# Holding the conversion and the fetch of a block of weights behind one more instruction of the step before

## The chip, the cores and the metric

The kernel runs on one core of one Trainium2 chip. That core has five engines that work side by side, each through its own list of instructions in its own order: TensorE (PE, matrix products), VectorE (DVE), ScalarE (ACT), GpSimd (POOL) and SyncE (SP, which here only issues transfers). The metric is the device time of one execution in microseconds (us), lower is better. Before the change it is 1103.98 us, the median of three runs (1102.27 to 1105.51).

## The reference

The program is an attention with a sliding window, followed by a two-layer network. There are 8 batches of 576 positions and 8 heads of 64 dimensions, so 4608 tokens of 512 numbers; everything is float32 at the output.

```
scores = q @ k.T / sqrt(64) - slope[head] * |rel|,  only where 0 <= rel < 128
attn   = exp(scores - max) / sum
x      = (attn @ v), heads side by side            # 4608 x 512
h      = x @ w_in                                  # 512 x 2048
g      = h if h >= 1;  0 if h <= -1;  (h+1)^2/4 between
out    = g @ w_out                                 # 2048 x 512
```

The two weight matrices arrive as float64. The kernel receives each of their numbers as two 32-bit words and has to put a float32 together from them before a matrix product can use it.

## The kernel before, in words

The 4608 tokens are cut into 12 chunks of 384 (`CH`); within a chunk the hidden size of 2048 is cut into 16 blocks of 128 (`NFC`), and block `fc` of chunk `c` is one step. A step does `layer1` (12 products of 128x384 into one PSUM bank `h`, then the activation: one ScalarE instruction that writes `sg`, two VectorE instructions that write `g`) and, two steps later, `layer2` (products of 128x512 that add into `acc`). The attention works by heads `m`, eight to a chunk: `scores` (products `s`, a VectorE pass at L249 that scales and takes the minimum into `z`, an exponential on ScalarE at L251, sums at L257 and L258, the fold of the two halves into `ep` at L262 or L264), `weights_t` (a transpose `p` on TensorE, a copy `lu` on ScalarE, two masks on GpSimd) and `values` (products `x`, a copy to `xn`). While the network runs on chunk `c`, the attention of chunk `c + 1` is put between its steps. The attention of chunk 0 has nothing ahead of it and stands alone at the start.

**The weights.** Block `fc` of a weight matrix is fetched by `fetch_weights(fc)`: two transfers of 512 KB that ScalarE's queue issues (L123 for `rawi`, L129 for `rawo`). `convert_in(fc)` makes the first layer's block of `rawi`, `convert_out(fc)` the second layer's of `rawo`. Both go through `float32_of`: two ScalarE instructions that scale the raw words in place (L112, L113), then three on VectorE (L114, L115, L116). `convert_in` adds a rounded copy on ScalarE (L135) and a remainder on VectorE (L136). All 16 blocks of both matrices are fetched and converted once, and must be ready for the 16 steps of chunk 0.

**What sets the order.** A scheduler writes each engine's list: of the instructions whose inputs it believes ready, it places the most urgent one first. The engines then follow their lists strictly. The only hand on it here is `behind(instructions, f)`: everything that `f` issues is placed, on the engine of each given instruction, behind that instruction. It orders one engine's list and nothing else. An instruction of `f` on an engine that has no instruction among those given is not held at all. The blocks 0 to 3 are converted behind heads of chunk 0's attention: `EARLY` names the heads, and `done_t[m]` holds the last instructions of `weights_t(m)`. The blocks 4 to 15 are converted by `convert_after`, one to a step of chunk 0: with `LEAD` = 4 it fetches block `f + 6` and converts block `f + 4` (for the second layer, behind the step before) behind `done_g[f]`, which holds instructions of the activation of step `f`.

Before the change `done_t[m]` of the first 16 heads holds a ScalarE and a GpSimd instruction, and `done_g[f]` the last VectorE instruction alone.

Of the kernel before, what the change touches and what calls it, by code (L numbers as in the profile page):

```python
# [12 lines left out]
AF = mybir.ActivationFunctionType  # L13
ALU = mybir.AluOpType
# [4 lines left out]
def windowed_attention_then_ffn(  # L19
# [21 lines left out]
    V, S, G, T, DMA = nc.vector, nc.scalar, nc.gpsimd, nc.tensor, nc.sync  # L41
# [4 lines left out]
    P = 128  # L46
# [31 lines left out]
    quarter = const.tile([P, 1], F32, name="quarter")  # L78
# [141 lines left out]
    def scores(m, blks):  # L220
        p, j = divmod(m, 2)
        c = p // NPAIR
        ql, kr, kk, kl = (pair[p].get(x) for x in ("ql", "kr", "kk", "kl"))
        if m not in head:
            head[m] = dict(ep=ap1.tile([P, NQB, P], F32, name=f"ep_{m}", tag="ep", bufs=2),
                           z=ap1.tile([P, NQB, 2 * P], F32, name=f"z_{m}", tag="z"),
                           nmax=ap1.tile([P, 4], F32, name=f"nmax_{m}", tag="nmax", bufs=2),
                           sum=sums[:, m % 2])
        st = head[m]
        nmax, sm, ep, z = st["nmax"], st["sum"], st["ep"], st["z"]  # L230
        slope = 2.0 ** -(m % H + 1)
        pt = bank(f"s_{m}_{blks[0]}").rearrange("r (m w) -> r m w", w=2 * P)
        b0 = before(c)
        win = []
        for n, i in enumerate(blks):
            lone = i + b0 == 0
            c0 = P if lone else D if c % CYCLE == 1 and i == 2 else 0
            k0 = (i + b0 - 1) * P + c0
            o = pt[:, n, c0:]
            win.append((o, c0, lone))  # L240
            if c < LIGHT:
                r, qs, ks = lo_rows[j], slice(i * P, (i + 1) * P), slice(k0, k0 + 2 * P - c0)
                T.matmul(o, ql[r, 0, qs].bitcast(F32), kr[r, 0, ks], start=True, stop=True)  # L243
                continue
            T.matmul(o, ql[:, j, i * P:(i + 1) * P], kk[:, j, k0:k0 + 2 * P - c0], start=True, stop=False)  # L245
            T.matmul(o, ql[:, j, i * P:(i + 1) * P], kl[:, j, k0:k0 + 2 * P - c0], start=False, stop=True)  # L246
        for i, (o, c0, lone) in zip(blks, win):
            r = rel_end if c % CYCLE == 1 and i == 1 else rel
            V.tensor_tensor_reduce(out=z[:, i, c0:], in0=o, in1=r[:, c0:], op0=ALU.add, op1=ALU.min, scale=-slope,  # L249
                                   scalar=3.0e38, accum_out=nmax[:, i:i + 1])  # L250
            S.activation(z[:, i, c0:], z[:, i, c0:], AF.Exp, bias=nmax[:, i:i + 1], scale=-1.0,  # L251
                         accum_out=sm[:, i, 0:1])
        if blks[-1] == NQB - 1:
            if c % CYCLE == 1:
                G.memset(z[:, 2, :D], 0.0)
            rc = st["rc"] = ap1.tile([P, 8], F32, name=f"rc_{m}", tag="rc", bufs=2)
            V.tensor_reduce(rc[:, :NQB], sm, mybir.AxisListType.X, ALU.add)  # L257
            V.reciprocal(rc[:, :NQB], rc[:, :NQB])  # L258

            for i in range(NQB):  # L260
                if i + b0 == 0:
                    V.tensor_tensor(ep[:, i, :], z[:, i, P:], rc[:, i:i + 1].broadcast_to([P, P]), ALU.mult)  # L262
                else:
                    V.tensor_tensor_reduce(out=ep[:, i, :], in0=z[:, i, :P], in1=z[:, i, P:], op0=ALU.add, op1=ALU.add,  # L264
                                           scale=rc[:, i:i + 1], scalar=0.0, accum_out=rc[:, 4 + i:5 + i])

    def weights_t(m):

        ep = head[m]["ep"]
        lu = head[m]["lu"] = ap1.tile([P, 2, 2 * NQB, P], F32R, name=f"lu_{m}", tag="lu", bufs=2)  # L270
        pt = bank(f"p_{m}")[:, :CH].rearrange("r (i w) -> r i w", w=P)
        for i in range(NQB):
            T.transpose(pt[:, i, :], ep[:, i, :], ident)  # L273
        if m < LIGHT * H:
            own = lu[:, 0, 1::2, :].bitcast(F32)
            ga = S.copy(own, pt)
            G.affine_select(out=lu[:, 0, 0::2, :].bitcast(F32), in_=own, pattern=[[0, NQB], [-1, P]],
                            base=0, channel_multiplier=1, compare_op=ALU.is_gt, fill=0.0)
            gg = G.affine_select(out=own, in_=own, pattern=[[0, NQB], [1, P]],
                                 base=0, channel_multiplier=-1, compare_op=ALU.is_ge, fill=0.0)  # L280
            done_t[m] = [ga.ins, gg.ins]
            return
        ga = S.copy(lu[:, 0, 1::2, :], pt)
        gv = V.tensor_tensor(lu[:, 1, 1::2, :], pt, lu[:, 0, 1::2, :].bitcast(F32), ALU.subtract)  # L284
        flat = lu.rearrange("p s i w -> p (s i) w")
        G.affine_select(out=flat[:, 0::2, :], in_=flat[:, 1::2, :].bitcast(F32), pattern=[[0, 2 * NQB], [-1, P]],  # L286
                        base=0, channel_multiplier=1, compare_op=ALU.is_gt, fill=0.0)
        gg = G.affine_select(out=flat[:, 1::2, :], in_=flat[:, 1::2, :].bitcast(F32), pattern=[[0, 2 * NQB], [1, P]],  # L288
                        base=0, channel_multiplier=-1, compare_op=ALU.is_ge, fill=0.0)
        done_t[m] = [ga.ins, gv.ins, gg.ins]  # L290
# [69 lines left out]
    def layer1(c, fc):  # L360
        ph = ps_h.tile([P, CH], F32, name=f"h_{c}_{fc}", tag="ps_h")
        for cc, (xh, xl) in enumerate(xs[c]):
            T.matmul(ph, wi[fc][:, 0, cc, :], xh, start=(cc == 0), stop=False)  # L363
            T.matmul(ph, wi[fc][:, 0, cc, :], xl, start=False, stop=False)  # L364
            T.matmul(ph, wi[fc][:, 1, cc, :], xh, start=False, stop=(cc == NCC - 1))  # L365

        if c == 0:
            g = gp.tile([P, CH], F32, name=f"g_{c}_{fc}", tag="gh")
        else:
            g = gp.tile([P, CH], F32, name=f"g_{c}_{fc}", tag="g", bufs=1)  # L370
        sg = gp.tile([P, CH], F32, name=f"sg_{c}_{fc}", tag="sg", bufs=1)
        S.activation(sg, ph, AF.Relu, bias=quarter[:, 0:1], scale=0.25)  # L372
        V.scalar_tensor_tensor(g, sg, 0.5, sg, ALU.min, ALU.mult)  # L373
        last = V.scalar_tensor_tensor(g, sg, -0.25, g, ALU.add, ALU.max)  # L374
        if c == 0:
            done_g[fc] = [last.ins]
            gs[c, fc] = g
            return
        gh = gp.tile([P, CH], F32R, name=f"gh_{c}_{fc}", tag="gh")
        gl = gp.tile([P, CH], F32R, name=f"gl_{c}_{fc}", tag="gl")  # L380
        S.copy(gh, g)  # L381
        G.tensor_tensor(gl, g, gh.bitcast(F32), ALU.subtract)  # L382
        gs[c, fc] = (gh, gl)
# [142 lines left out]
```

## Time and profile before

| | us |
|---|---|
| median of 3 runs | 1103.98 (1102.27 to 1105.51) |
| the profiled execution, its own time | 1102.24 |
| the span of its trace | 1100.5 |
| TensorE busy | 1045.3 (95%) |
| VectorE busy | 810.4 (74%) |
| ScalarE busy | 617.4 (56%) |
| GpSimd busy | 372.1 (34%) |

The span runs from the first instruction to the last; 1.74 us of the execution's own time lie around it. A busy share is a mean over stages that differ: the first tenth of the span, in which chunk 0's attention runs and the weights come in, looks unlike the rest. An engine's row in a timeline gives the start, the length, the line, the operation with out and in, and in brackets how long the engine stood idle before it and what ended that. The granted clock of TensorE (PEclk) is a share of its full speed.

### The profile page before, as it was taken

The numbers are of one execution on the slowest core, as the hardware profiler recorded it, in microseconds if no ns is written. First come the engines' busy times: TensorE is split into PE (matmuls) and PEld (weight loads), VectorE is DVE, ScalarE is ACT, GpSimd is POOL, SyncE is SP. The second block draws the span as 40 slices with busy tenths as digits, with TensorE's granted clock in tenths as the row PEclk, the third lists the DMA queues.
The fourth block names the chain that finished last, engine by engine and source line by source line (L and its number), as shares of the span: only waits on it lengthen the run. The fifth ranks groups of instructions, "written<-read, shape, count | busy, mean of one in ns | idle before, by whom it ended". The sixth has DMA issues, their size and how long they took to land.

```text
span 1100.5 us, 16790 instructions
## 1 busy us (share of the span) xinstructions
PE 1045.3 (95%) x5472; PEld 905.1 (82%) x5472; DVE 810.4 (74%) x2281; ACT 617.4 (56%) x1475; POOL 372.1 (34%) x419
## 2 busy tenths in 40 slices
PE   4489999999999999999999999999999999999998
PEld 2246666889899998899898898899899889899996
DVE  2458999978878878887887778897777897763322
ACT  3876335755656655655665655664665665652322
POOL 1011210433443343344344343444333444343221
PEclk9977999999999999999999999999999999999999
DMA  9722101221211312212121212211112221200000
GB/s 352 261 89 92 37 17 29 65 59 29 87 34 49 89 37 64 73 32 58 58 65 42 66 46 63 65 48 42 59 44 63 66 72 38 74 2 1 29 1 29
DMA packets 58903, 69.50 MB, mean 63 GB/s; under 512 B 4032, under 2 KB 44480, under 8 KB 58816
## 3 DMA queue, kind: packets, MB, share of 16 engines
q1 hardware_dynamic: 48064, 51.66, 16.3%
q10 hardware_dynamic: 10752, 16.78, 4.1%
q8 instruction: 43, 0.70, 0.3%
q14 instruction: 44, 0.36, 0.1%
HBM read 58.98 MB, written 9.44 MB: 62 GB/s over the span
## 4 chain that ended last, share of the span: by engine, by line
PE 80%; DVE 6%; ACT 6%; DMA 3%; issue 2%; POOL 2%; ACTq 0%; DVEq 0%; POOLq 0%
PE h L363 11%; PE h L364 11%; PE h L365 11%; PE acc L396 10%; PE acc L397 10%; PE acc L398 9%; PE x L338 5%; PE acc L393 4%; PE p L273 3%; PE s L246 2%; PE s L245 2%; PE x L314 2%; DMA rawi<-in_moe_w_in_dram 2%; PE s L243 2%; ACT z L251 1%
## 5 line engine op out<-in xcount | busy, mean ns | idle before, releaser
L382 POOL TENSOR_TENSOR gl<-g,gh 128x384 fp32r<-128x384 f32 x176 | 182.7, 1038 | 416.9 <-ACT gh L381 408.4
L363 PE MATMUL h<-xh,wi 128*128 128x384 f32 x768 | 265.9, 346 | 6.0 <-ACT xh L356 5.4
L364 PE MATMUL h<-xl,wi 128*128 128x384 f32 x768 | 261.1, 340 | 0.0
L365 PE MATMUL h<-xh,wi 128*128 128x384 f32 x768 | 259.8, 338 | 0.0
L396 PE MATMUL acc<-wo,gh 128*128 128x512 f32 x528 | 211.8, 401 | 5.7 <-ACT gh L381 5.7
L373 DVE SCALAR_TENSOR_TENSOR g<-sg 128x384 f32<-128x384 f32 x192 | 108.8, 567 | 140.9 <-ACT sg L372 121.7
L397 PE MATMUL acc<-wo,gh 128*128 128x512 f32 x528 | 207.9, 394 | 0.0
L372 ACT ACTIVATE sg<-h,quarter 128x384 f32<-128x384 f32 x192 | 111.0, 578 | 161.0 <-PE h L365 152.2
L381 ACT CAST gh<-g 128x384 fp32r<-128x384 f32 x176 | 90.3, 513 | 190.0 <-DVE g L374 178.8
L363 PEld LDWEIGHTS h<-xh,wi 128*128 128x128 f32 x768 | 144.7, 188 | 16.2 <-ACT xh L356 6.6
L251 ACT ACTIVATE z<-z,nmax 128x256 f32<-128x256 f32 (+2 forms) x288 | 139.1, 486 | 31.3 <-DVE nmax L249 23.2
L398 PE MATMUL acc<-wo,gl 128*128 128x512 f32 x528 | 155.8, 397 | 0.2 <-POOL gl L382 0.2
L364 PEld LDWEIGHTS h<-xl,wi 128*128 128x128 f32 x768 | 144.8, 189 | 7.2 <-issue 2.5
L365 PEld LDWEIGHTS h<-xh,wi 128*128 128x128 f32 x768 | 144.8, 189 | 0.0
L264 DVE CUSTOM_DVE_ANT_0 ep<-z,rc 128x128 f32<-128x128 f32 x256 | 128.6, 543 | 1.4
L286 POOL TENSOR_SCALAR_AFFINE_SELECT lu<-lu 128x768 fp32r<-128x768 f32 x80 | 82.2, 1028 | 139.6 <-DVE lu L284 132.2
L249 DVE CUSTOM_DVE_ANT_0 z<-s,rel 128x256 f32<-128x256 f32 (+2 forms) x256 | 93.9, 394 | 45.9 <-PE s L246 37.0
L396 PEld LDWEIGHTS acc<-wo,gh 128*128 128x128 f32 x528 | 99.4, 188 | 24.8 <-ACT gh L381 8.0
L374 DVE SCALAR_TENSOR_TENSOR g<-sg,g 128x384 f32<-128x384 f32 x192 | 112.1, 584 | 3.2
L398 PEld LDWEIGHTS acc<-wo,gl 128*128 128x128 f32 x528 | 97.2, 188 | 19.7 <-POOL gl L382 0.4
L397 PEld LDWEIGHTS acc<-wo,gh 128*128 128x128 f32 x528 | 99.4, 188 | 16.5
L288 POOL TENSOR_SCALAR_AFFINE_SELECT lu<-lu 128x768 fp32r<-128x768 f32 x80 | 80.8, 1010 | 4.7
(80 smaller groups left out, 1488.1 us busy)
## 6 DMA issues: line engine op xcount, KB each, us to landing
kr<-in_k_dram SPq DMA_DIRECT2D x60, 256.0 KB, 3.8
qr<-in_q_dram SPq DMA_DIRECT2D x48, 192.0 KB, 3.5
out_dram<-o SPq DMA_DIRECT2D x36, 256.0 KB, 2.9
rawi<-in_moe_w_in_dram ACTq DMA_DIRECT2D x16, 512.0 KB, 8.8
rawo<-in_moe_w_out_dram ACTq DMA_DIRECT2D x16, 512.0 KB, 8.7
vn<-in_v_dram SPq DMA_DIRECT2D x32, 256.0 KB, 2.7
kr<-in_k_dram SPq DMA_DIRECT2D x28, 192.0 KB, 3.3
vn<-in_v_dram SPq DMA_DIRECT2D x16, 192.0 KB, 2.5
```

The costliest lines, as they stand in the source:

```text
L251: S.activation(z[:, i, c0:], z[:, i, c0:], AF.Exp, bias=nmax[:, i:i + 1], scale=-1.0, accum_out=sm[:, i, 0:1])
L264: V.tensor_tensor_reduce(out=ep[:, i, :], in0=z[:, i, :P], in1=z[:, i, P:], op0=ALU.add, op1=ALU.add, scale=rc[:, i:i + 1], scalar=0.0, ac ...
L363: T.matmul(ph, wi[fc][:, 0, cc, :], xh, start=(cc == 0), stop=False)
L364: T.matmul(ph, wi[fc][:, 0, cc, :], xl, start=False, stop=False)
L365: T.matmul(ph, wi[fc][:, 1, cc, :], xh, start=False, stop=(cc == NCC - 1))
L372: S.activation(sg, ph, AF.Relu, bias=quarter[:, 0:1], scale=0.25)
L373: V.scalar_tensor_tensor(g, sg, 0.5, sg, ALU.min, ALU.mult)
L374: last = V.scalar_tensor_tensor(g, sg, -0.25, g, ALU.add, ALU.max)
L382: G.tensor_tensor(gl, g, gh.bitcast(F32), ALU.subtract)
L396: T.matmul(a, gh[:, ts], wo[fc][:, 0], start=first, stop=False)
L397: T.matmul(a, gh[:, ts], wo[fc][:, 1], start=False, stop=False)
L398: T.matmul(a, gl[:, ts], wo[fc][:, 0], start=False, stop=last)
```

## The change

Two lists of instructions get one more entry each. `done_g[f]` gets the ScalarE instruction that writes `sg` of step `f`, beside the VectorE one that it had; so the ScalarE part of a fetch and of a conversion (L112, L113, L135 and the issue of the two transfers) is held behind it. `done_t[m]` of the first 16 heads gets the last VectorE instruction of the fold of that head; so the VectorE part of the first four blocks' conversion is held behind it. No instruction is added or taken away by it and no size changes.

```diff
@@ in scores(m, blks)
                 else:
-                    V.tensor_tensor_reduce(out=ep[:, i, :], in0=z[:, i, :P], in1=z[:, i, P:], op0=ALU.add, op1=ALU.add,
+                    st["folded"] = V.tensor_tensor_reduce(out=ep[:, i, :], in0=z[:, i, :P], in1=z[:, i, P:], op0=ALU.add, op1=ALU.add,
                                            scale=rc[:, i:i + 1], scalar=0.0, accum_out=rc[:, 4 + i:5 + i])
@@ in weights_t(m), m < LIGHT * H
-            done_t[m] = [ga.ins, gg.ins]
+            done_t[m] = [head[m]["folded"].ins, ga.ins, gg.ins]
@@ in layer1(c, fc)
-        S.activation(sg, ph, AF.Relu, bias=quarter[:, 0:1], scale=0.25)
+        first = S.activation(sg, ph, AF.Relu, bias=quarter[:, 0:1], scale=0.25)
         V.scalar_tensor_tensor(g, sg, 0.5, sg, ALU.min, ALU.mult)
         last = V.scalar_tensor_tensor(g, sg, -0.25, g, ALU.add, ALU.max)
         if c == 0:
-            done_g[fc] = [last.ins]
+            done_g[fc] = [first.ins, last.ins]
```

Where it moves instructions, three places show. In the names, the number behind `rawi` and `rawo` tells blocks apart: 125 and 127 are block 0, 129 and 131 block 1, 626 and 628 block 6, 692 and 694 block 7, 924 and 926 block 11, 1038 and 1040 block 13.

ScalarE at the start, from the exponentials of head 1 (`z_154`) to those of head 2 (`z_190`). Before:

```order
L251 ACTIVATE z_154,sums<-z_154,nmax_155 128x256
L123 DMA rawi_924<-in_moe_w_in_dram 128x4x256
L129 DMA rawo_926<-in_moe_w_out_dram 128x1024
L112 ACTIVATE rawi_626<-rawi_626 128x512
L113 ACTIVATE rawi_626<-rawi_626 128x512
L123 DMA rawi_983<-in_moe_w_in_dram 128x4x256
L129 DMA rawo_985<-in_moe_w_out_dram 128x1024
L123 DMA rawi_1038<-in_moe_w_in_dram 128x4x256
L112 ACTIVATE rawo_628<-rawo_628 128x512
L113 ACTIVATE rawo_628<-rawo_628 128x512
L129 DMA rawo_1040<-in_moe_w_out_dram 128x1024
L251 ACTIVATE z_190,sums<-z_190,nmax_191 128x128
```

Now:

```order
L251 ACTIVATE z_154,sums<-z_154,nmax_155 128x128
L276 COPY lu_179<-p_180 128x3x128
L251 ACTIVATE z_154,sums<-z_154,nmax_155 128x256 x2
L193 ACTIVATE ql_173<-qr_121,qscale 128x384
L251 ACTIVATE z_190,sums<-z_190,nmax_191 128x128
```

The fetches of the blocks 11 to 13 and the conversion of block 6 that stood between two heads are gone from there; head 2 follows head 1 directly.

ScalarE in chunk 0's steps, from the activation of step 2 (`sg_2`) to that of step 3. Before:

```order
L372 ACTIVATE sg_2_740<-h_2_726,quarter 128x384
L251 ACTIVATE z_817,sums<-z_817,nmax_818 128x256 x2
L251 ACTIVATE z_817,sums<-z_817,nmax_818 128x192
L276 COPY lu_840<-p_841 128x3x128
L135 CAST wi_702<-f_i_696 128x512
L372 ACTIVATE sg_3_792<-h_3_778,quarter 128x384
```

Now:

```order
L372 ACTIVATE sg_2_740<-h_2_726,quarter 128x384
L123 DMA rawi_744<-in_moe_w_in_dram 128x4x256
L129 DMA rawo_746<-in_moe_w_out_dram 128x1024
L112 ACTIVATE rawi_626<-rawi_626 128x512
L113 ACTIVATE rawi_626<-rawi_626 128x512
L112 ACTIVATE rawo_694<-rawo_694 128x512
L113 ACTIVATE rawo_694<-rawo_694 128x512
L135 CAST wi_702<-f_i_696 128x512
L251 ACTIVATE z_817,sums<-z_817,nmax_818 128x256 x2
L251 ACTIVATE z_817,sums<-z_817,nmax_818 128x192
L372 ACTIVATE sg_3_792<-h_3_778,quarter 128x384
```

Two transfers of block 8, the scaling of `rawi` of block 6 and that of `rawo` of block 7 now stand between the two activations; `lu_840` has moved behind `sg_3`.

TensorE at the start, behind the transpose of head 0 (`p_180`). Before:

```order
L273 MATMUL p_180<-ident,ep_133 128x128 x3
L243 MATMUL s_0_192<-kr_123,ql_173 128x128
L243 MATMUL s_0_192<-kr_123,ql_173 128x256
L243 MATMUL s_2_199<-kr_123,ql_173 128x256
L314 MATMUL x_231<-lu_179,vn_117 64x256 x2
L314 MATMUL x_231<-lu_179,vn_117 64x128
```

Now:

```order
L273 MATMUL p_180<-ident,ep_133 128x128 x3
L314 MATMUL x_231<-lu_179,vn_117 64x256 x2
L314 MATMUL x_231<-lu_179,vn_117 64x128
L243 MATMUL s_0_192<-kr_123,ql_173 128x128
L243 MATMUL s_0_192<-kr_123,ql_173 128x256
L243 MATMUL s_2_199<-kr_123,ql_173 128x256
```

The values of head 0 (`x_231`) have moved ahead of the scores of head 2 (`s_0_192`, `s_2_199`). On VectorE the conversions of the blocks 0 to 3 keep their places behind the folds of the heads, with a few neighbours exchanged. The lists of GpSimd differ in a few neighbours, that of SyncE not at all; from the second chunk on the lists of all engines become the same again.

## The prediction

> **What bounds the kernel now.** I read the slices of the page first, then the busy time by stretches, then the waits of VectorE and ScalarE in the stretch that stands out.
>
> ```profile
> PE   4489999999999999999999999999999999999998
> ...
> ACT  3876335755656655655665655664665665652322
> ...
> PEclk9977999999999999999999999999999999999999
> ```
>
> TensorE fills its slices except for the first three (27.5 us each), and its granted clock is low in the third and fourth. So the bulk is TensorE's and the start is somebody else's.
>
> ```profile
> 20.00:30.00 10.00, 6.26 (x17) 3.13 (x15) 2.85 (x18) 5.67 (x14) 0.00 (x0) 1.00 1.06 401
> ...
> 40.00:50.00 10.00, 3.21 (x8) 1.48 (x6) 4.83 (x8) 10.00 (x20) 0.00 (x0) 1.00 0.54 200
> ...
> 70.00:80.00 10.00, 10.00 (x25) 5.59 (x24) 3.10 (x15) 5.35 (x14) 1.25 (x3) 0.50 0.24 72
> ...
> 200.00:300.00 100.00, 98.58 (x558) 89.83 (x558) 84.93 (x239) 62.18 (x150) 40.46 (x39) 1.00 0.18 57
> ```
>
> The columns are the stretch, its length, the busy time of PE, PEld, DVE, ACT and POOL, PEclk, the share of the transfer engines and GB/s. From 20 to 30 us the transfers are full (401 GB/s), from 40 to 50 ScalarE is (10.00 of 10), from 70 to 80 TensorE is, at half clock. Later TensorE is busy 98.58 of 100 at full clock. A saving in the start is therefore kept to the end, as long as chunk 0 does not give it back.
>
> I set a milestone that both lists of VectorE share: the end of the fold of head 9, at 93.60 us.
>
> ```profile
> 8.30:93.60 85.30, 55.03 (x146) 30.45 (x143) 39.59 (x160) 60.39 (x146) 10.20 (x20) 0.86 0.62 224
> 98.58:170.19 71.61, 71.61 (x295) 46.61 (x295) 68.19 (x178) 27.86 (x70) 11.71 (x17) 1.00 0.11 31
> ```
> ```profile
> DVE rc L257 <- ACT z L251: 24.3, 8, 6.9
> DVE z L249 <- PE s L243: 7.3, 6, 3.7
> DVE f_i L114 <- ACT rawi L112: 5.5, 1, 5.5
> DVE xl L357 <- ACT xh L356: 4.4, 2, 2.5
> DVE wi L136 <- ACT wi L135: 2.5, 2, 1.4
> ```
>
> Between the first scores (8.30) and the milestone VectorE works 39.59 of 85.30 us. It waits mostly for ScalarE: 24.3 us for exponentials, 5.5 for the first scaled weights, 4.4 and 2.5 for rounded copies. And ScalarE is late for two reasons:
>
> ```profile
> ACT z L251 <- DMA rawo<-in_moe_w_out_dram: 4.0, 1, 4.0
> ACT rawi L112 <- DMA rawo<-in_moe_w_out_dram: 2.7, 1, 2.7
> ACT rawo L112 <- DMA rawo<-in_moe_w_out_dram: 2.0, 1, 2.0
> ACT z L251 <- DMA rawi<-in_moe_w_in_dram: 1.2, 1, 1.2
> ```
> ```profile
> L112 ACT ACTIVATE rawi<-rawi 128x512 f32<-128x512 f32 x16 | 10.5, 655 | 5.9 <-issue 3.2 <-DMA rawo<-in_moe_w_out_dram 2.7
> ...
> L112 ACT ACTIVATE rawo<-rawo 128x512 f32<-128x512 f32 x15 | 9.9, 663 | 2.4 <-DMA rawo<-in_moe_w_out_dram 2.0 <-issue 0.4
> ```
> ```profile
> 41.06 0.66 ACT L113 ACTIVATE rawi<-rawi 128x512 int32<-128x512 uint32 x1
> 41.62 0.65 ACT L112 ACTIVATE rawo<-rawo 128x512 f32<-128x512 f32 x1
> ```
>
> It stands 9.9 us behind issues of fetches (4.0, 2.7, 2.0 and 1.2), and it scales 31 blocks (16 of `rawi`, 15 of `rawo`), each L112 followed by an L113, one instruction every 0.56 us (41.06 to 41.62): 31 x 2 x 0.56 = 34.7 us of its 60.39. Most of these belong to blocks that no step needs before 100 us.
>
> **The change, part by part.**
>
> *ScalarE at the start, removed.* By the new list only 7 of those 31 pairs come before the milestone (`rawi` of the blocks 0 to 3, `rawo` of 0 to 2). So 24 x 2 x 0.56 = 26.9 us of ScalarE work and the 9.9 us behind the transfers leave the start, and ScalarE keeps 60.39 - 26.9 = 33.5 us there. That is less than VectorE's 39.6, so VectorE's own chain is late next. What does that chain need?
>
> ```profile
> 81.72 0.42 DVE L249 CUSTOM_DVE_ANT_0 z<-s,rel 128x256 f32<-128x256 f32 x1
> ...
> 83.81 0.16 DVE L257 TENSOR_REDUCE rc<-sums 128x3 f32<-128x6 f32 x1 [1.03 <-ACT z L251]
> ...
> 84.77 0.35 DVE L264 CUSTOM_DVE_ANT_0 ep<-z,rc 128x128 f32<-128x128 f32 x1
> ...
> 93.60 0.56 DVE L357 TENSOR_TENSOR xl<-xn,xh 128x384 fp32r<-128x384 f32 x1
> ...
> 95.04 0.69 DVE L136 TENSOR_TENSOR wi<-f_i,wi 128x512 fp32r<-128x512 f32 x1
> ```
>
> Head 8 runs undisturbed: 81.72 to 85.12, of which 1.03 us is the wait for its last exponential. There is one `z`, so heads follow each other and each pays that wait. The new list has two more instructions ahead of the milestone, an L357 (0.56) and an L136 (0.69). Work is thus 39.6 + 1.2 = 40.8 us. The idle time has two bounds. The least is 10 heads x 1.03 = 10.3 us; the milestone then falls at 8.3 + 40.8 + 10.3 = 59.4, a gain of 34.2. The most that the rows leave is that the other waits stay as they are, 7.3 + 4.4 + 2.5, beside the 10.3: 24.5, milestone 73.6, gain 20.0. I take 14 us: of the extra waits, those for `xh` and `wi` are ScalarE's lateness and go, and half of the 7.3 for scores stays, because on TensorE the values of head 0 now stand ahead of the scores of head 2. Milestone 63.1, **gain 30.5 us**.
>
> *ScalarE in chunk 0, added.* The 26.9 us come back between the activations of the steps 0 to 11.
>
> ```profile
> 98.58 0.60 ACT L372 ACTIVATE sg<-h,quarter 128x384 f32<-128x384 f32 x1
> ...
> 170.19 0.58 ACT L372 ACTIVATE sg<-h,quarter 128x384 f32<-128x384 f32 x1 [0.60 <-PE h L365]
> ```
> ```profile
> ACT sg L372 <- PE h L365: 20.1, 7, 5.1
> ```
>
> From `sg` of step 0 to that of step 11 take 71.61 us, 6.5 a step. ScalarE is busy 27.86 of them and would be 54.8, still below; 20.1 us of its idle time is waiting for `h`, and that is the cover. Behind each activation now stand two issues and four scalings (2.24 us), and behind these the exponentials, which VectorE's sums wait for, and the next activation, which TensorE waits for, since `h` has one bank. Bounds: 0 with the cover, 26.9 if all of it is exposed. VectorE is busy 68.19 and TensorE 71.61 of 71.61, so there is little slack to absorb a late exponential: I take **a loss of 4 us**, nearer to the covered end because ScalarE has 16.8 us (71.6 - 54.8) left.
>
> *The fetches, moved.* Twenty issues leave the start and stand behind `sg` of step f, for a block converted two steps (13 us) later.
>
> ```profile
> rawi<-in_moe_w_in_dram ACTq DMA_DIRECT2D x2, 512.0 KB, 3.6
> rawo<-in_moe_w_out_dram ACTq DMA_DIRECT2D x2, 512.0 KB, 4.6
> ```
>
> Issued between 60 and 100 us, when little else moves, such a block lands in 3.6 and 4.6 us: hidden, cost 0; with the cover gone it would be 4.6 a step. SyncE's list is unchanged; its loads of q, k and v lose their competitor at the start, which I count as part of the gain above.
>
> *VectorE behind `folded`.* The conversions of the blocks 0 to 3 stood behind these folds already; cost 0, with the 1.2 us above as the one shift.
>
> *TensorE's clock.* A wait can cost more than its length:
>
> ```profile
> 87.40 2.40 PE L314 MATMUL x<-lu,vn 128*64 128x256 f32 x6 [1.06 <-POOL lu L279]
> ```
> ```profile
> 84.00:86.00 2.00, 2.00 (x10) 1.00 0.00 0
> 86.00:88.00 2.00, 0.94 (x5) 0.73 0.56 170
> 88.00:90.00 2.00, 2.00 (x7) 0.50 1.07 399
> ```
>
> After an idle 1.06 us the clock falls to 0.50. Chunk 0 has run at 1.00 without a wait; I count no fall. [...] By the trace the sum could lose more, which is the third rival.
>
> The sum: 1102.24 - 30.5 + 4 = 1075.7 for an execution like the profiled one, which lies 1.74 below the median; for the median 1077.5, and I write **1077 us**.
>
> **The rivals.**
>
> *Chunk 0 gives half of it back* (circular waits). ScalarE, VectorE and TensorE are then all near full and wait for each other in order. For it: VectorE 68.19 of 71.61. Against it: ScalarE's spare 16.8 us. Price 26.9 / 2 = 13.5 instead of 4: 1087.
>
> *The start is VectorE's and TensorE's chain, not ScalarE's.* Then only the 9.9 us behind the transfers are won, less the 4: 1098. For it: the 7.3 us for scores at half clock. Against it: 24.3 us for exponentials.
>
> *Slower: the clock falls in chunk 0.* One mechanism: a late exponential or activation makes TensorE wait about 1 us, and the clock stays at 0.50 for some 10 us, as from 87 on, which costs about 5 us a fall. From 6 falls in the 16 steps the gain of 26.5 is gone; with ten it is 1077 + 50 = 1127. Against it: twelve dense products in each step, and that a TensorE at half speed is behind and no longer waits.
>
> *The change binds nothing.* The lists show it does at both places, but the list is no time: if the start were held by transfers alone, 1104.
>
> **How the numbers follow.** Forecast 0.62 (own range 1070 to 1084: a gain of 34.2 without loss, or one of 24 with 4); half given back 0.22; the chain 0.08; slower 0.05; nothing 0.03. To leave at most 2 in 10 out I go from 1067, a little below the forecast's best since the heads' own waits might shrink too, to 1092, which takes in the half given back. What a measurement tells from no change is 0.3%, about 3.3 us: faster 0.62 + 0.22 + 0.08 = 0.92, same 0.03, slower 0.05.
>
> **What would show it.** The fold of head 9 ends near 63 us; transfers run full for the first 10 us alone; no L112 stands between the exponentials of the heads 0 to 2; VectorE's wait for exponentials there falls from 24.3 to some 10 us; steps 0 to 11 take about 75 us with L112 between all activations; PEclk is 1.0 from about 70 us on. I am wrong if the milestone stays beyond 74, or if steps 0 to 11 take over 85.

## The result, and the profile after

The changed kernel takes 1067.65 us (median of four runs, 1066.38 to 1070.27); the kernel before took 1103.12 us beside it (1100.33 to 1105.51). The ratio is 0.9682, with a 95% interval of 0.9652 to 0.9713. In a second comparison the same two kernels gave 1068.89 and 1099.48 us, a ratio of 0.9724 (0.9700 to 0.9747). The profiled execution took 1067.44 us, 34.8 us less than the profiled one of before. I had forecast 1077 and, between the profiled executions, a gain of 26.5.

The page of the changed kernel, its span, busy times and slices (26.6 us each):

```profile
span 1065.7 us, 16820 instructions
...
PE 1031.5 (97%) x5472; PEld 899.5 (84%) x5472; DVE 810.6 (76%) x2281; ACT 617.9 (58%) x1475; POOL 375.5 (35%) x419
...
PE   6899999999999999999999999999999999999998
...
ACT  4777667556556556557565556656565655742322
...
PEclk9989999999999999999999999999999999999999
```

Before, the first three slices of TensorE read 4, 4 and 8; now 6, 8 and 9. The page holds a second account of the gain that I had not drawn up. Span less busy time is TensorE's idle time: 1100.5 - 1045.3 = 55.2 us before, 1065.7 - 1031.5 = 34.2 now. So 21.0 us of the gain are idle time that has gone, and 13.8 us are the same 5472 rows of products taking less time, that is, running at a higher rate. (Of some products the trace has two rows each, of the added ones below for instance. "Six values products" are six such rows.)

The busy time of the engines by stretches (columns as in the prediction):

```profile
10.00:20.00 10.00, 6.88 (x19) 4.32 (x20) 4.41 (x26) 4.03 (x16) 1.05 (x2) 1.00 0.29 97
20.00:30.00 10.00, 10.00 (x26) 5.29 (x26) 7.98 (x33) 7.98 (x22) 2.09 (x4) 1.00 0.75 258
...
25.00:30.00 5.00, 5.00 (x14) 2.90 (x13) 4.12 (x18) 5.00 (x15) 1.04 (x2) 1.00 1.03 363
...
40.00:50.00 10.00, 8.20 (x36) 4.73 (x36) 8.15 (x36) 6.00 (x19) 2.63 (x5) 1.00 0.33 110
...
70.00:80.00 10.00, 10.00 (x46) 7.03 (x45) 10.00 (x28) 7.49 (x18) 2.13 (x3) 1.00 0.60 209
```

From 10 to 20 us the transfers move 97 GB/s, where they were full until 45 us before (387 to 405 GB/s from 5 us on); from 25 to 30 us they are full once more (363 GB/s). ScalarE is busy 6.00 of 10 from 40 to 50 us instead of 10.00. From 70 to 80 us TensorE and VectorE are both busy 10.00 of 10. TensorE's granted clock is 1.00 there; before it was 0.50.

My milestone, the end of the fold of head 9, has moved from 93.60 to 60.05 us (the row behind that fold on VectorE), and `sg` of step 0 on ScalarE from 98.58 to 59.43, that of step 11 from 170.19 to 133.82:

```profile
60.05 0.56 DVE L373 SCALAR_TENSOR_TENSOR g<-sg 128x384 f32<-128x384 f32 x1
```
```profile
59.43 0.58 ACT L372 ACTIVATE sg<-h,quarter 128x384 f32<-128x384 f32 x1 [0.98 <-PE h L365]
...
133.82 0.58 ACT L372 ACTIVATE sg<-h,quarter 128x384 f32<-128x384 f32 x1 [1.77 <-PE h L365]
```

Between the first scores and the milestone, and from step 0 to step 11, the stretches read as follows. Behind them stand VectorE's waits up to the milestone, all that it has:

```profile
8.20:60.05 51.85, 42.53 (x149) 24.14 (x147) 39.80 (x164) 34.27 (x99) 10.74 (x20) 0.98 0.49 166
59.43:133.82 74.39, 74.32 (x302) 50.27 (x303) 69.38 (x195) 55.16 (x119) 12.63 (x18) 0.96 0.51 171
```
```profile
DVE z L249 <- PE s L243: 7.6, 5, 3.6
DVE rc L257 <- ACT z L251: 6.5, 8, 1.3
```

VectorE does the same work up to the milestone (39.80 us, 39.59 before) in 51.85 instead of 85.30 us. Its wait for exponentials has fallen from 24.3 to 6.5 us; those for weights and rounded copies are gone. ScalarE's work there fell from 60.39 to 34.27 us, and in the steps 0 to 11 it rose from 27.86 to 55.16 us. The conversion's scalings ahead of the milestone are the seven that the lists show, and the fetches land as quickly as forecast:

```profile
L112 ACT ACTIVATE rawi<-rawi 128x512 f32<-128x512 f32 x4 | 2.7, 678 | 0.5 <-issue 0.5
...
L112 ACT ACTIVATE rawo<-rawo 128x512 f32<-128x512 f32 x3 | 2.0, 677 | 0.0
```
```profile
rawo<-in_moe_w_out_dram ACTq DMA_DIRECT2D x10, 512.0 KB, 4.5
rawi<-in_moe_w_in_dram ACTq DMA_DIRECT2D x9, 512.0 KB, 3.7
```

Counted from the milestone to the first output nothing is given back in sum: the first output is issued 104.65 us after it before (198.25) and 103.42 us after it now (163.47). What this sum is made of stands below, under "Chunk 0".

### The profile page after: what moved, and what is told of

Same layout as the page of the kernel before. It is cut to its first block, busy times and chain, and to the rows that moved or that the text cites. A ratio compares the mean times of both kernels' runs of the same rounds, so it can differ in the third digit from the quotient of the medians.

```text
span 1065.7 us, 16820 instructions
## 1 busy us (share of the span) xinstructions
PE 1031.5 (97%) x5472; PEld 899.5 (84%) x5472; DVE 810.6 (76%) x2281; ACT 617.9 (58%) x1475; POOL 375.5 (35%) x419
## 4 chain that ended last, share of the span: by engine, by line
PE 81%; DVE 9%; ACT 5%; issue 3%; POOL 2%; DMA 0%; ACTq 0%; DVEq 0%; POOLq 0%
PE h L363 11%; PE h L364 11%; PE h L365 11%; PE acc L396 10%; PE acc L397 10%; PE acc L398 9%; PE x L338 5%; PE acc L393 4%; PE p L273 3%; PE s L246 2%; PE s L245 2%; PE x L314 2%; PE s L243 2%; ACT z L251 1%; DVE g L373 1%
## 5 line engine op out<-in xcount | busy, mean ns | idle before, releaser
L382 POOL TENSOR_TENSOR gl<-g,gh 128x384 fp32r<-128x384 f32 x176 | 183.7, 1044 | 412.4 <-ACT gh L381 406.6
```

## The experiments

My theory was: 26.9 us of scaling and 9.9 us of standing behind transfers leave ScalarE's list at the start, and in the steps of chunk 0 ScalarE's idle time covers what comes back. The rivals: the gain is the transfers', not ScalarE's; or it is TensorE's rate; or the start is now bound by something else than I thought.

All edits are to the changed kernel. One table for all of them. The ratio is to the kernel before on the same chip, as recorded; it can differ by some 0.2% from the ratio of the medians. "Head 9" is the start of the sum (L257) of head 9, some 2 us ahead of the milestone and easy to find in every list; "steps" is from `sg` of step 0 to that of step 11; "chunk 1" is from the first output of chunk 0 to the first of chunk 1.

| kernel | median us | ratio, 95% | head 9 | `sg` 0 | steps | chunk 1 | TensorE busy / idle |
|---|---|---|---|---|---|---|---|
| before | 1103.12 | | 91.85 | 98.58 | 71.6 | 82.7 | 1045.3 / 55.2 |
| changed | 1067.65 | 0.9682 (0.9652 to 0.9713) | 57.72 | 59.43 | 74.4 | 83.1 | 1031.5 / 34.2 |
| changed, again | 1068.89 | 0.9724 (0.9700 to 0.9747) | 59.97 | 61.79 | 73.8 | 83.0 | 1036.1 / 32.5 |
| fetch free | 1089.97 | 0.9889 (0.9859 to 0.9918) | 83.33 | 87.55 | 74.6 | 83.0 | 1049.3 / 46.8 |
| conversion free | 1072.27 | 0.9749 (0.9711 to 0.9787) | 63.17 | 72.42 | 67.9 | 82.6 | 1035.6 / 34.5 |
| half of the fetches free | 1069.53 | 0.9710 (0.9684 to 0.9737) | 62.09 | 63.92 | 73.0 | 81.7 | 1031.3 / 36.5 |
| fetches on SyncE, 4 to 15 | 1103.02 | 1.0027 (1.0010 to 1.0044) | 85.62 | 87.67 | 74.3 | 91.1 | 1042.6 / 59.4 |
| fetches on SyncE, 2 to 15 | 1089.63 | 0.9898 (0.9872 to 0.9925) | 75.31 | 77.56 | 72.8 | 82.8 | 1040.9 / 46.9 |
| more ScalarE work | 1080.17 | 0.9818 (0.9780 to 0.9855) | 59.19 | 62.02 | 72.0 | 93.4 | 1038.5 / 40.6 |
| less VectorE work | 1077.08 (of three; a fourth took 3538.23) | 0.9803 (0.9776 to 0.9831) | 58.55 | 64.63 | 70.3 | 90.7 | 1039.1 / 35.6 |
| remainder on GpSimd | 1083.21 | 0.9840 (0.9807 to 0.9872) | 64.66 | 66.71 | 72.3 | 91.4 | 1046.6 / 38.6 |
| copy on ScalarE | 1072.11 | 0.9735 (0.9709 to 0.9760) | 57.71 | 64.02 | 68.4 | 85.0 | 1034.6 / 35.6 |
| warm | 1065.23 | 0.9681 (0.9654 to 0.9708) | 57.25 | 60.08 | 72.2 | 83.0 | 1038.4 / 26.1 |
| warm, fetch free | 1089.71 | 0.9906 (0.9878 to 0.9935) | 80.85 | 85.26 | 70.5 | 83.0 | 1051.1 / 36.9 |

The columns from "head 9" on are read from one profiled execution of each kernel. That of "fetch free" took 1097.99 us, the longest of six and 8.0 above the median, so its later columns are those of a long execution; that of "remainder on GpSimd" took 1086.93, 3.7 above its median (1078.70 to 1086.93). All others lie within 1.7 us.

The column "chunk 1" has two kinds of kernel: most at 82 to 85 us and four at 91 to 93. In those four the scheduler's lists differ from the changed kernel's not in chunk 0 alone, but for two thirds of the program, until about 732 us. (The lists of the changed kernel itself meet those of before at 212 us in its trace, in the middle of chunk 1 and not at its start.) They lose 8 to 10 us in chunk 1, where none of them changes anything. So of those four I read the columns up to "steps", not the median.

One question needed no run, since the lists answer it. With the entry `folded` left out, the lists of all five engines are word for word those of the changed kernel; with this entry alone they are those of the kernel before. The whole effect is that of the entry that holds work behind `sg`.

### The changed kernel again

> The changed kernel once more, to stand beside the others on the same chip: 0.965 to 0.971 of the kernel before, about 1065 where that takes 1100. A ratio outside this would mean that the smaller differences between the experiments say nothing.

Measured: 1068.89 us, a ratio of 0.9724, outside the band by 0.0014 with an interval that reaches 0.9700. So differences between experiments of less than 4 to 5 us say nothing. The profiled execution of this run is 2.9 us longer than the first (span 1068.6 to 1065.7) with the same lists. At the first output it is 1.8 us behind (165.26 to 163.47). TensorE at the start, in the first and in the second:

```profile
28.13 2.39 PE L314 MATMUL x<-lu,vn 128*64 128x256 f32 x6
...
34.03 1.30 PE L314 MATMUL x<-lu,vn 128*64 128x256 f32 x6
...
57.79 0.44 PE L363 MATMUL h<-xh,wi 128*128 128x384 f32 x1 [1.05 <-ACT xh L356]
```
```profile
26.81 1.30 PE L314 MATMUL x<-lu,vn 128*64 128x256 f32 x6
...
32.68 0.69 PE L364 MATMUL h<-xl,wi 128*128 128x384 f32 x1 [1.90 <-DVE xl L357]
...
34.04 2.40 PE L314 MATMUL x<-lu,vn 128*64 128x256 f32 x6
```

Six values products take 2.39 or 1.30 us, which I call half and full rate (in the second execution the granted clock reads 0.50 from 34 to 42 us and 1.00 from 44 to 56). By these rows full rate begins behind 30.5 us in the first execution and by 26.8 us in the second. There a wait of 1.90 us follows, the rate falls at 32 and comes back at 42, and head 9 is 2.25 us later. The other 1.1 us come later.

### The two halves of the hold

The diff against the changed kernel, first the fetch let go, then the conversion:

```diff
-                behind(done_g[f], lambda: fetch_weights(fc + 2))
+                behind(done_g[f][1:], lambda: fetch_weights(fc + 2))
```

> The conversions stay held behind the activation as in the changed kernel; only the fetches are let go again on ScalarE's queue, so that all of them stand between the heads of chunk 0 as before the change. My theory (the gain is 26.9 us of scaling work plus up to 9.9 us in which ScalarE stands behind issues): the 9.9 us come back and nothing else, milestone (end of the fold of head 9) at 65 to 70 instead of 60.05, time 1073 to 1078. Rival, transfers hold the start: nearly the whole gain is lost, milestone beyond 85, time 1095 or more. Rival, the scaling alone was the cause: milestone within 1 us of 60.05, time 1066 to 1070.

```diff
-            behind(done_g[f], lambda: convert_in(fc))
-            behind(done_g[f - 1 if f else f], lambda: convert_out(fc))
+            behind(done_g[f][1:], lambda: convert_in(fc))
+            behind(done_g[f - 1 if f else f][1:], lambda: convert_out(fc))
```

> The fetches stay held as in the changed kernel; the ScalarE part of the conversions is let go, held only by the VectorE part as before the change. By the new list only the blocks 4 and 5 are scaled ahead of the activation of step 0, each later one about a step earlier than in the changed kernel. My theory: a late fetch alone keeps the scaling away from the start, so the hold on the conversions adds nothing beyond it: milestone at 60 to 65 (up to four pairs of scalings, 4.5 us, ahead of it), time 1066 to 1072. Rival, the hold on the conversions carries the gain: time 1085 or more, milestone beyond 75.

Measured: 1089.97 us with the fetch free, which lies in none of the three ranges, and 1072.27 with the conversion free. Holding the conversion alone is worth 1.1% of the time before (12 us, 10 by the medians), holding the fetch alone 2.5% (28 us), both together 2.8 to 3.2% (30 to 35). The 28 are not the transfers' alone, because a block that comes late is also scaled late. The clean step is from the free fetch to the changed kernel, with the scalings held in both: 21 to 22 us. My theory falls on its first half. It gave the fetches 9.9 us; they carry some two thirds of the gain. With them back, the 26.9 us of scaling taken from the start bought only 10 to 12, and ScalarE's waits from 8 to 42 us in the version with free fetches show why:

```profile
ACT z L251 <- issue: 11.7, 3, 7.8
ACT z L251 <- DMA rawo<-in_moe_w_out_dram: 4.2, 1, 4.2
ACT rawi L112 <- issue: 2.4, 1, 2.4
...
ACT z L251 <- DMA rawi<-in_moe_w_in_dram: 1.2, 1, 1.2
```

It stands 19.5 us at issues where it stood 14.7 in the same stretch before (the 9.9 of the prediction and 4.8 named "issue"). So the scalings of before had, it seems, in part stood in time that ScalarE would have waited anyway. On top of the fetch's hold that of the conversion adds 3.4 to 4.6 us, which is not clear of the 4 to 5 us above: the late fetch alone keeps most of the scalings away from the start, as expected (its time lies 0.3 us above the range written down).

### Who issues the fetches, and how many

Is it ScalarE's standing, or the full transfers? Two kernels move the issue to SyncE's queue, where nothing holds it:

```diff
-        S.dma_start(w1, wi32[...])
+        (S if fc < 4 else DMA).dma_start(w1, wi32[...])
...
-        S.dma_start(w2, wo32[...])
+        (S if fc < 4 else DMA).dma_start(w2, wo32[...])
```

> The fetches of the blocks 4 to 15 go to SyncE's queue, where nothing holds them: they stand early, among the loads of q, k and v. ScalarE's list has none of them between the heads, so no exponential stands behind one, and the conversions stay held. Theory A, the early fetches hurt by making ScalarE stand behind their issue (19.6 us before 40 us in the run with free fetches): gone here, time 1065 to 1073, VectorE's wait for exponentials in 8 to 90 us below 10 us. Theory B, they hurt by filling the transfers until about 37 us, which makes the loads of q and k and the blocks 0 to 3 late whoever issues: milestone beyond 75, TensorE at half clock from about 30 to 90 us, time 1083 to 1095.

The second one has `fc < 2` in the same places.

> The fetches of the blocks 2 to 15 all go to SyncE's queue, early; in the earlier run with the blocks 4 to 15 there, ScalarE still stood 15.2 us at its own issue of block 2. Here it issues nothing after the first 7 us and can only wait for data. Theory A, ScalarE standing at issues is what the early fetches cost: no such wait left, milestone 60 to 68, time 1066 to 1074. Theory B, the transfers full until about 37 us make the loads of q, k and v late that stand behind them: VectorE waits for scores (over 10 us) and TensorE for scaled q, milestone over 72, time 1078 or more.

The first told the theories apart badly. VectorE's wait for exponentials was 6.9 us, as theory A wanted, but ScalarE stood once more behind fetches, now at its own issue of block 2, and the time, 1103.02, lies above both ranges (8.0 us of it are lost in chunk 1, as said):

```profile
ACT rawi L112 <- DMA rawo<-in_moe_w_out_dram: 17.9, 2, 15.2
```

In the second ScalarE stands at no issue from 8 to 42 us, and yet the time is 1089.63, the same as with free fetches on ScalarE. Theory A falls: head 9 is at 75.31, outside its 60 to 68. What is late now are the loads that stand behind the fetches in SyncE's list. The fourth load of `kr` is issued at 41.96 us, behind the last fetch:

```profile
39.89 1.97 SPq L129 DMA_DIRECT2D rawo<-in_moe_w_out_dram  x1
41.96 0.38 SPq L172 DMA_DIRECT2D kr<-in_k_dram  x1
```

In the changed kernel the same load is issued at 22.65 us. The waits that follow from it (VectorE's, ScalarE's and TensorE's from 8 to 90 us):

```profile
DVE z L249 <- PE s L243: 21.6, 12, 8.9
```
```profile
ACT ql L193 <- DMA qr<-in_q_dram: 7.0, 2, 6.2
```
```profile
PE x L314 <- DMA vn<-in_v_dram: 6.0, 1, 6.0
```

So a queue of early fetches holds up whatever stands behind it: on ScalarE the exponentials (17.1 us of waits between 8 and 42 us with free fetches), on SyncE the loads of q, k and v (the fourth `kr` at 41.96 for 22.65 us). That the transfers are full is the smaller part, as far as the traces show: in the kernel before, whose transfers move 397 GB/s from 5 to 45 us, the loads of q, k and v that SyncE issues between 8 and 42 us land in the median 5.1 to 6.6 us behind their issue, in the changed kernel 2.7 to 4.3. How much it costs depends on how many fetches there are. Half of them let go:

```diff
-                behind(done_g[f], lambda: fetch_weights(fc + 2))
+                behind(done_g[f][1:] if f < 5 else done_g[f], lambda: fetch_weights(fc + 2))
```

> Only the fetches of the blocks 6 to 10 are let go again on ScalarE's queue (ten transfers of 512 KB, 5.2 MB), those of the blocks 11 to 15 stay held as in the changed kernel. With all ten blocks free the time is 1089.97 and the transfers are full from 10 to about 42 us; with none 1067.65 to 1068.89. If the price is set by how long the transfers are full (by bytes): full until about 27 us, half of the 22 us, 1076 to 1081, milestone at 70 to 75. Rival, the transfers have room for some blocks (they move only 97 of some 400 GB/s from 10 to 20 us in the changed kernel): 1066 to 1071. Rival, a few early gaps are enough, because they take TensorE's full rate away for the rest of the start: 1084 or more.

Measured: 1069.53 us, within the spread of the changed kernel. The price is not in proportion to the bytes: five blocks cost nothing that can be told, ten cost 21 us. The transfers are full from 5 to 25 us, then they ebb:

```profile
20.00:25.00 5.00, 5.00 (x14) 2.75 (x13) 2.95 (x19) 2.03 (x9) 0.00 (x0) 1.00 1.07 401
25.00:30.00 5.00, 4.45 (x13) 2.08 (x13) 3.81 (x13) 4.64 (x12) 2.09 (x4) 1.00 0.94 319
30.00:35.00 5.00, 4.37 (x21) 2.63 (x19) 4.78 (x10) 2.93 (x6) 0.00 (x0) 1.00 0.87 292
```

Head 1's sum is 5 us late there (18.90 instead of 13.84), head 9's 4.4 and `sg` of step 11 only 3.1 (136.88). The lag of the early heads is made up later; that of ten blocks is not. Why it turns between five and ten I have not tried.

### Is it TensorE's rate?

With free fetches TensorE is the busy engine of the later start, and at half rate, in the long execution that the trace shows:

```profile
60.00:70.00 10.00, 10.00 (x28) 6.19 (x26) 5.81 (x28) 5.30 (x17) 2.40 (x5) 0.50 0.27 86
70.00:80.00 10.00, 10.00 (x27) 5.59 (x26) 4.30 (x22) 5.77 (x18) 1.20 (x3) 0.50 0.26 87
```

That could be the cause, or a consequence. The edit adds 44 products whose results nobody uses (its lines are rearranged here for reading):

```diff
+    warm = ps_h.tile([P, CH], F32, name="warm", tag="ps_h")
     make_identity(nc, ident)
+    for _ in range(20): T.matmul(warm[:, :P], ident, ident, start=True, stop=True)
...
+        for _ in range(10 if m == 0 else 0): T.matmul(warm[:, :P], ident, ident, start=True, stop=True)
         for i in range(NQB): T.transpose(pt[:, i, :], ep[:, i, :], ident)
...
         b0 = before(c)
+        for _ in range(14 if m == 0 else 0): T.matmul(warm[:, :P], ident, ident, start=True, stop=True)
```

> Added to the changed kernel: 44 products of the identity with itself (128x128, 0.22 us each at half rate, result unused): 20 before the first scores, while TensorE waits for q and k until 6.5 us, and 24 in its gaps between 9.6 and 20 us. Two executions of the changed kernel showed TensorE at half rate until 30.5 and until 25.5 us (six values products take 2.39 us, later 1.30). If the rate at the start sets the pace of the first heads: six values products take 1.30 us already before 20 us, milestone 2 to 5 us earlier than 60 to 62, time 1060 to 1065. Rival, the first heads wait for VectorE, ScalarE and GpSimd in turn and TensorE only has longer gaps (or falls back to half rate in them): 1066 to 1070. Rival, the added products delay the transposes behind them: over 1070.

> The same 44 products in the version whose fetches are let go on ScalarE's queue (1090, TensorE at half rate until about 97 us, of which it is busy all the time from 60 us on). If the half rate itself, caused only by the late first 30 us, is the price of the early fetches: full rate from 20 us on, milestone below 72, time 1072 to 1080. Rival, the gaps that the fetches tear between 15 and 40 us bring the half rate back at once, whatever went before: no full rate at 50 to 90 us, 1086 to 1092.

In the changed kernel the products did what they should. TensorE begins at 1.64 (20 products, two rows each, in 7.21 us), and the twelve rows of the first scores take 1.68 us where they took 3.09. All values products from 20 to 41 us take 1.30:

```profile
1.64 7.21 PE L77 MATMUL warm<-ident 128*128 128x128 f32 x40 [1.64 <-POOL ident masks.py:199]
8.78 1.68 PE L243 MATMUL s<-kr,ql 64*128 64x128 f32 x12
...
20.39 1.29 PE L314 MATMUL x<-lu,vn 128*64 128x256 f32 x6
...
41.22 1.30 PE L314 MATMUL x<-lu,vn 128*64 128x256 f32 x6 [0.79 <-POOL lu L279]
...
49.65 2.40 PE L314 MATMUL x<-lu,vn 128*64 128x256 f32 x6
```

The time did not follow: 1065.23 us, a ratio of 0.9681 where the changed kernel had 0.9682 and 0.9724. It lies at the seam of two expectations and can't be told from no gain. It is the lowest median of all, but not shown to beat the changed kernel. So the rate of the first 40 us does not set the pace of the changed kernel, beyond the 4 to 5 us that these runs can't tell. With free fetches the added products bring nothing at all (1089.71 against 1089.97). But there they did not keep the rate: behind a wait of 5.10 us, which ends at 19.81, the products are slow again (two rows of scores take 1.22 us at 21.77, 0.70 at 19.76 with the fetches held), and the granted clock is 0.50 from 20 to 30 us. The rival had this, though not the 0.95 that is read from 70 to 80. So a full rate before 20 us is not enough there; what a rate kept through the gaps would bring, this run does not show. That the 13.8 us of faster products only come along with the closed gaps is therefore argued, not shown.

### What binds the start now

> Left out: one VectorE instruction (the sign's, L115) in the conversion of the blocks 0 to 3, so these weights lack their sign; 8 instructions of 0.69 us, 7 of them ahead of the milestone, 4.8 us less VectorE work there and nothing else changed. If the start is now VectorE's chain: milestone 3.5 to 5 us earlier, time 1060 to 1063. Rival, VectorE's waits for the exponentials and scores (14.1 us) grow by what its work shrinks: milestone within 1 us of 60.05, time 1065 to 1068.

```diff
-        V.scalar_tensor_tensor(fi, high, -0x80000000, fi, ALU.bitwise_and, ALU.bitwise_or)
+        if int(name[1:]) >= 4:
+            V.scalar_tensor_tensor(fi, high, -0x80000000, fi, ALU.bitwise_and, ALU.bitwise_or)
```

Head 9's sum stands at 58.55 us, between the two executions of the changed kernel (57.72 and 59.97), and `sg` of step 0 later than in both. Up to the milestone, which stands at 59.77, VectorE works 6.9 us less (32.95 for 39.80), and its idle time has grown by 6.6: the rival. As far as this run shows, VectorE is not what sets the start now. But TensorE came to full rate later in this execution (six values products still take 1.70 us at 36.27), and that may hide a gain. The time, above both ranges, is that of a kernel whose lists differ far on.

> The subtraction that makes the remainder of a first-layer block goes from VectorE to GpSimd for all 16 blocks: VectorE gets 0.69 us lighter per block, 4 of these blocks (2.8 us) in the start and 12 (8.3 us) in the steps of chunk 0. GpSimd has the time, it is busy 2.5 of 10 us there. If the start is now VectorE's chain, as I put it: milestone 2 to 3 us earlier and, since VectorE is full from 70 to 100 us too, 1058 to 1064. Rival, what binds now is TensorE with its order of waits: 1065 to 1068. Rival, GpSimd's slower subtraction makes the products of the first layer wait: over 1069.

```diff
         S.copy(t[:, 0], f)
-        V.tensor_tensor(t[:, 1], f, t[:, 0].bitcast(F32), ALU.subtract)
+        G.tensor_tensor(t[:, 1], f, t[:, 0].bitcast(F32), ALU.subtract)
```

Head 9's sum is at 64.66 us, 5 to 7 later, and the time over 1069 as the third expectation had it. GpSimd's subtraction is the slower one (1.02 us in the median for 128x384 at L382 of the changed kernel, where VectorE takes 0.55 at L357), but that is not what shows. Six values products still take 2.39 us at 47.21 and 2.40 at 57.59, the half rate, although TensorE is almost never idle:

```profile
30.00:40.00 10.00, 10.00 (x30) 6.03 (x30) 7.96 (x20) 6.62 (x17) 4.44 (x6) 1.00 0.45 135
...
50.00:60.00 10.00, 10.00 (x26) 5.68 (x25) 5.19 (x28) 6.26 (x20) 2.51 (x6) 1.00 0.22 66
```
```profile
57.59 2.40 PE L314 MATMUL x<-lu,vn 128*64 128x256 f32 x6
61.32 1.30 PE L314 MATMUL x<-lu,vn 128*64 128x256 f32 x6
```

Here the rate seems to set the pace, with 10.00 of 10 busy from 50 to 60 us at 2.40 us for six rows; no run of its own tests it. What brings the rate back and when stays open.

> The copy of one group of the attention's values (group 3 of each chunk) goes from VectorE to ScalarE, which has the lighter load; it stands ahead of the rounded copy that TensorE waits 1.05 us for at 57.8, after which its clock is half until about 65.5. If that wait is what costs (3.5 us at half clock and 1 us of waiting): clock at 1.00 through 58 to 66, time 1063 to 1065. Rival, a TensorE at half clock there is behind VectorE anyway, or the wait moves elsewhere: time 1066 to 1069.

```diff
-                    (V.tensor_copy if g % 2 else S.copy)(xn[c, g], px)
+                    (V.tensor_copy if g == 1 else S.copy)(xn[c, g], px)
```

Inconclusive. The edit moves the copy in chunk 0 alone, not in each chunk as the expectation says, and 1072.11 lies above both of its ranges. The fall of the rate moved instead of going away (six products take 1.69 us at 53.66 already; the granted clock is 0.72 from 50 to 60 and 0.94 from 60 to 70 us, where it was 0.91 and 0.74). Step 11 is reached 1.4 us earlier than in the changed kernel (132.40), and 4.7 us are lost between there and the first output of chunk 1; why, I have not tried.

### Is ScalarE's idle time in the steps the cover?

> One more ScalarE instruction (a multiplication by 1.0 in place) in every conversion of the blocks 4 to 15: 24 of them at 0.56 us, 13.4 us more of ScalarE work in the steps of chunk 0 and none at the start. If ScalarE's idle time in the steps covers what the change put there (the reading of why chunk 0 lost nothing after the milestone), this is covered as well: time within 2 us of the changed kernel's 1067.65, steps 0 to 11 at 74.4 to 76.5 us. Rival, the cover was just used up: most of the 13.4 us show, time 1075 to 1081, steps 0 to 11 at 82 us or more.

```diff
         S.mul(high.bitcast(F32), high.bitcast(F32), 2.0 ** -112)
         S.activation(low, low.bitcast(U32), AF.Copy, scale=2.0 ** -29)
+        if int(name[1:]) >= 4:
+            S.mul(high.bitcast(F32), high.bitcast(F32), 1.0)
```

The time, 1080.17, looks like the rival's. The place does not. The steps 0 to 11, where all of the added work stands, took 72.0 us, no more than in the changed kernel: covered. The loss comes later, 6.0 us between step 11 and the first output and 10.4 in chunk 1, and starts with a wait of TensorE for GpSimd:

```profile
145.67 2.82 PE L316 MATMUL x<-lu,vn 128*64 128x256 f32 x8 [4.36 <-POOL lu L281]
```

This is one of the four kernels whose lists differ far into the program, so the loss is put down to the lists, not to ScalarE's load; that is argued, not shown by a run of its own.

## Why the prediction was right, and where it was wrong

**The number.** 1067.65 and 1068.89 us lie at the lower end of the wide range, 1067 to 1092, and below the forecast's own, 1070 to 1084, whose best case was the best milestone without any loss. So the gain was underrated, and the pieces below show that some of the fit is luck.

**The milestone.** Forecast 63.1 (a gain of 30.5, bounds 20.0 and 34.2), measured 60.05 (33.55), near the best bound. The work was 39.8 us for 40.8 forecast; VectorE's waits add up to 14.1 us for the 14 that I took, of which 12.05 are idle time by the stretch's busy column. But the sum is right with wrong parts. I put 10.3 us on exponentials and half of 7.3 on scores; it was 6.5 on exponentials, less than the "10 heads x 1.03 = 10.3" that I took for the least, and 7.6, the whole, on scores. That the total of 14 came out is luck. That the values of head 0 stand ahead of the scores of head 2 did not shorten that wait.

**Which cause it was.** "24 x 2 x 0.56 = 26.9 us of ScalarE work and the 9.9 us behind the transfers leave the start" is true as an account of ScalarE (60.39 to 34.27 us of work). As an account of causes it failed: the two do not add up, since ScalarE without scalings stood longer at the issues (19.5 us for 14.7). The fetches are the larger part, and the runs on SyncE show that not ScalarE's standing alone counts, but what stands behind a full queue of transfers, on either engine. The rival "only the 9.9 us behind the transfers are won", 1098, was wrong in the same way, from the other side.

**Chunk 0.** Forecast a loss of 4 us behind the milestone; measured a gain of 1.2. The mechanism, ScalarE's idle time as a cover, held (55.16 us of ScalarE work in the steps, 54.8 forecast), and the run with 13.4 us more of it speaks for it too. But the sum lacked a piece, and the piece that it had came out for another reason. The activation of step 0 stood 4.98 us behind the milestone before and stands 0.62 us ahead of it now: 5.6 us won that I had not counted. From step 0 to the first output 4.4 us are lost, close to the 4 that I wrote down for late exponentials and activations. They are not that. The steps 0 to 11 took 74.39 us, "about 75" as said, 2.8 more than before; the granted clock over this stretch is 0.96, and 74.39 x 0.96 = 71.4 us is about what they took before (71.61). From step 11 to the first output it is 1.6 us more, with 120 rows of products where there were 111, and TensorE busy nearly all the time in both, before and now:

```profile
170.19:198.25 28.06, 27.88 (x111) 18.94 (x110) 26.13 (x61) 18.60 (x41) 1.25 (x1) 1.00 0.16 43
```
```profile
133.82:163.47 29.65, 29.60 (x120) 19.85 (x119) 27.65 (x63) 20.35 (x45) 1.88 (x3) 1.00 0.15 40
```

So the loss of 4 was right by luck. The lower clock is there because the steps start 6 us ahead of where the rate comes back:

```profile
60.00:62.00 2.00, 2.00 (x6) 1.21 (x7) 1.96 (x8) 1.59 (x4) 0.15 (x1) 0.50 0.65 177
...
66.00:68.00 2.00, 2.00 (x10) 1.37 (x9) 1.45 (x8) 1.91 (x4) 1.29 (x3) 1.00 0.16 30
```

The 3.05 us at the milestone and the 5.6 between it and step 0, less some 0.4 by which the later loss exceeds 4, make up the 8.3 us by which the gain exceeded the forecast.

**The clock.** "I count no fall" in chunk 0 was right from 66 us on, and the third rival fell. But I did not count what the change gives back in rate: the same products take 13.8 us less. It did not spoil the sum, because that was made on VectorE's chain and not on TensorE's busy time.

**Fetches at 0, `folded` at 0** held: 4.5 and 3.7 us to land, and identical lists. Half given back, slower, and no effect did not come.

**The marks that I named.** The fold of head 9 at 60.05 for "near 63"; no L112 between the exponentials of the heads 0 to 2 (the first stands at 22.50 us, behind head 2's last at 19.79); VectorE's wait for exponentials 6.5 for "some 10"; steps about 75; full rate from 66 us for "about 70". These came. Transfers full for the first 10 us alone came in part: 97 GB/s behind that, but full once more from 25 to 30 us.

## What to carry to other kernels

Work and waits in one in-order list need not add up: take the work away and the engine may stand at the next issue for longer, as ScalarE did here (19.5 us for 14.7), so a saving counted as so many instructions of such a length needs the question what the engine would do in that time. Prefetches that nothing needs for 100 us are not free when they stand ahead of loads and issues that somebody needs now; a few hid themselves here (five blocks), ten cost 21 us. And where a scheduler writes the lists, compare them to the end of the program before a small difference is explained: four of these kernels lost 8 to 10 us in a chunk that the edit did not touch.

## What the runs showed of the hardware

The granted clock in the stretches was not to be trusted at the start of these executions. In the kernel before, six values products take 2.40 us at 33.06, where the column says 1.00 from 30 to 40 us; so the low rate that I read in the third and fourth slice was there earlier. From 20 to 30 us the changed kernel's row says 1.00, while six values products take 2.39 us at 28.13; with the fetches of the blocks 4 to 15 on SyncE it says 1.00 up to 80 us, and the same six take 2.40 at 70.66:

```profile
60.00:70.00 10.00, 9.32 (x25) 5.57 (x25) 6.50 (x27) 3.71 (x12) 1.20 (x2) 1.00 0.10 32
```
```profile
70.66 2.40 PE L314 MATMUL x<-lu,vn 128*64 128x256 f32 x6
```

The length of a known product was the better clock here.

Full rate began behind 30.5 us in one execution of the changed kernel and by 26.8 in another, so the point of change varied by at least 3.7 us between two executions of the same lists. Behind 7.2 us of back-to-back identity products it had come (the twelve rows of the first scores take 1.68 us there, 3.09 without them). In the kernel with the remainder on GpSimd TensorE is shown busy for 9.46 to 10.00 of every 10 us from 20 to 60 us, and six values products took 2.39 us at 28.06 and at 47.21 and 2.40 at 57.59 (the twelve rows at 38.46 took 3.31, less than twice that). What sets the point of change, no run here shows.

The rate fell at waits of 1.05 us (57.79, the changed kernel) and 1.90 us (32.68, its second execution) and stayed at half for some 7 and 10 us; a wait of 0.86 us (37.72, the first execution) had no fall behind it, nor had one of 1.06 us with the copy on ScalarE (38.08).
